# Block-sparse attention and a GELU MLP on one core: weights loaded between batch 0 and batch 1, masks of batch 1 turned by TensorE, casts on GpSimd, key sums from the key transposes

## The chip, the core and the metric

The kernel runs on one core of one Trainium2 chip. The metric is the time of the whole program on the device in microseconds, as the median of several runs. Beside it stands one profiled execution, which gives start, length and waits of every instruction. A compute core has five engines that run side by side, each working through its own instructions in order: TensorE (PE in the profile; its weight loads are PEld), VectorE (DVE), ScalarE (ACT), GpSimd (POOL) and SyncE (SP), which here only issues transfers. An engine that waits for one instruction holds up everything behind it.

## What is computed

Block-sparse causal attention over 4 batches, 8 heads, 768 positions and head width 64, followed by a two-layer MLP without biases:

```python
k_rep = k.reshape(B, H, 12, 64, D).mean(axis=3)          # one key mean per block of 64
gate_scores = einsum('bhsd,bhnd->bhsn', q, k_rep)        # per query and block
gate_scores = where(causal, gate_scores, -1e9)
top_idx = argsort(gate_scores)[..., -3:]                 # the 3 best blocks
mask = (chosen blocks, and the own block) & (i >= j)
scores = where(mask, q @ k.T / sqrt(D), -1e9)
attn = softmax(scores)
x = (attn @ v), heads side by side                       # 3072 x 512
h = x @ w_in                                             # 3072 x 2048
out = gelu_tanh(h) @ w_out                               # 3072 x 512
```

q, k, v, w_in, w_out and the output are fp32. The kernel multiplies in fp16 but takes the gate scores in fp32, since they decide which blocks are chosen.

## The kernel before, in words

Two heads make a pair; there are 16 pairs, four to a batch, so pair 4 is the first of batch 1. For each pair `pre` (line 342) prepares, `heads2` (batch 0) or `heads` (batches 1 to 3) computes the attention, and `turn_out` (673) turns the normalised result into xT, the MLP's input. For each batch `s1` (791) is the first MLP layer with GELU (128 matmuls, of 512 and of 256 columns in turn, L798) and `s2` (822) the second (96 matmuls, L829). s1 of a batch starts when the last exponential of its attention is done; the attention of the next batch starts when nearly all of s1 has been multiplied. s2 of one batch is filler for TensorE during the attention of the next.

*No order is written out by hand.* Every piece of work is an `Op` with a cost for each engine that may do it, its dependencies, a priority, and the PSUM bank it takes. `Plan.solve` (52) simulates all engines by these costs, takes the ready operation of the best priority at each step, picks the engine that ends first, and emits all operations in the order of their planned starts. So a changed cost changes the order of many instructions and the engine of some. The costs are plans only; on the chip an instruction waits for its real operands, in the fixed order of its engine.

*Loading.* `load` (215) issues k, q and v of a pair from SyncE. Pairs of batch 0 come in rows of 64 values and are turned by TensorE (`turn`, 351, into PSUM, with copies out of it in `turned`). Later pairs come as blocks of 32 x 32 in four transfers each for k and q (`emit_t`), and DVE's 32 x 32 transpose (`tr`, 374, shown as L378) finishes the turn. k and q have four buffers each, v three.

*Key sums and gates.* In batch 0 the sums of each block of 64 keys are six more fp32 matmuls a pair with an indicator matrix `ind` (L361), behind the second half of the key transposes. In later batches DVE adds them up (`ks_all`, L400). `ksb_m` (L418) spreads them over the two heads, `gate` (L455) multiplies them with the queries, DVE turns the scores (L468) and picks the three best blocks (`sel_e`, L474 to 487), which leaves an additive mask, `madd`.

*Masks.* The mask must be turned so that it can stand beside the queries as extra rows. In batch 0 TensorE does it (`mask`, L508), in the later batches a transposing DMA from SyncE (`mask_dma`, L516), and `mc` copies twelve rows for each head into qT.

*Casts.* `cast_v` makes v fp16 on DVE. The fp16 casts of keys (`kc_all`) and queries (`q16`) go to DVE or ScalarE.

*Attention.* Scores (L589, L729), exponential on ScalarE (L603, L742), the causal triangle cut by GpSimd (L629, L756), multiplication with v (L642, L768), and normalisation on DVE (L667, L668).

*Weights.* `load_w` (258) issues them from GpSimd, with a cast to fp16 during the transfer: w_in in two parts during batch 0, w_out in one piece when v of pair 5 has arrived. A small copy of v, `after` (L264), makes GpSimd wait for that arrival. `hold` (271) is a tiny transfer from SyncE that reads the first part of w_in; it holds SyncE's queue, and so all loads of batch 1, until that part is there.

*Warm-up.* `warm` (859) offers 110 matmuls without use of the worst priority, with which TensorE passes the time while it has nothing else.

Of the kernel before, what the change touches and what calls it, by code (L numbers as in the profile page):

```python
# [8 lines left out]
FP32 = mybir.dt.float32  # L9
# [113 lines left out]
def kernel(  # L123
# [22 lines left out]
    HALF = S // 2  # L146

# [15 lines left out]
    ident32 = const.tile([128, 128], FP32)  # L163
# [3 lines left out]
    bmask = const.tile([128, 2, 16], FP32)  # L167
    nc.vector.memset(bmask, 0.0)
# [6 lines left out]
    ks16 = [const.tile([128, 16], FP32, name=f"ks16_{i}") for i in range(NK)]  # L175
    for i in range(NK):
        nc.vector.memset(ks16[i], 0.0)
    start = gtp.tile([128, NF, S], FP16, tag="gT", name="start")
# [36 lines left out]
    def load(p, key, held=None, prio=None):  # L215
        b, hp = divmod(p, HP)

        def emit(_):
            sd = (iov if key == "v" else io).tile(
                [128, NC, 2, 64], FP32, tag=key, name=f"{key}_sd_{p}")  # L220
            for hh in range(2):
                nc.sync.dma_start(
                    out=sd[:, :, hh, :],
                    in_=SRC[key][b, 2 * hp + hh].rearrange(
                        "(c p) d -> p c d", p=128))
            T[key, p] = sd
        def emit_t(_):

            sd = io.tile([128, NC * 4, 32], FP32, tag=key, name=f"{key}_sd_{p}")
            for hh in range(2):  # L230
                for a in range(2):
                    nc.sync.dma_start(  # L232
                        out=sd[64 * hh + 32 * a:64 * hh + 32 * a + 32],
                        in_=SRC[key][b, 2 * hp + hh].rearrange(
                            "(t i) (a j) -> a i t j", i=32, j=32)[a])
            T[key, p] = sd
        dve = key != "v" and p >= HP
        go = add({SP: 2.0 if dve else 1.0}, emit_t if dve else emit,
                 [free_sd.get((key, p - (PV if key == "v" else PF))), held]
                 + moved[-3:-2],  # L240
                 prio=10 * p if prio is None else prio)
        issued[key, p] = go
        ld[key, p] = add({"DMA": 2.5 if dve else 1.8},
                         lambda _: None, [go],
                         prio=1000 * b + hp, lag=1.6)
        moved.append(ld[key, p])

    def cast_v(p, old):
        b, hp = divmod(p, HP)

        def emit(eng):
            copy(eng, v16[p % NB][:, :, :, 0:64], T["v", p])
        free_sd["v", p] = ld["v16", p] = add(
            {DVE: 0.47}, emit,
            [ld["v", p], old],
            prio=1000 * (b - 1) + 599 + hp if b else 100 * hp - 55)

    def load_w(name, dst, src, cols, deps, prio, after=None):
        view = src.rearrange("(i p) f -> p i f", p=128)

        def emit(_):
            if after is not None:
                x = const.tile([1, 16], FP32, name="after")
                nc.gpsimd.tensor_copy(out=x, in_=T[after][0:1, 0, 0, 0:16])  # L264
            nc.gpsimd.dma_start(out=dst[:, :, cols], in_=view[:, :, cols])
        go = add({POOL: 1.3}, emit, deps, prio=prio)
        n = dst.shape[1] * (cols.stop - cols.start)
        return add({"DMA": 12.0 * n / 8192}, lambda _: None, [go], prio=prio,
                   lag=1.6)

    def hold(dep):
        def emit(_):
            x = const.tile([1, 16], FP16, name="held")
            nc.sync.dma_start(out=x, in_=w_in16[0:1, 0, 0:16])
        return add({SP: 0.5}, emit, [dep], prio=-1)
# [3 lines left out]
    def consts():  # L279
        def ind(_):  # L280
            T["ind"] = x = const.tile([128, NC, 16], FP32, name="ind")
            nc.gpsimd.memset(x, 1.0)
            nc.gpsimd.affine_select(
                out=x, in_=x, compare_op=ALU.is_ge, fill=0.0,
                base=0, pattern=[[128, NC], [-64, 16]], channel_multiplier=1)
            nc.gpsimd.affine_select(
                out=x, in_=x, compare_op=ALU.is_ge, fill=0.0,
                base=63, pattern=[[-128, NC], [64, 16]], channel_multiplier=-1)
        c_E["ind"] = add({POOL: 1.2}, ind, [], prio=-60)

# [51 lines left out]
    def pre(p):  # L342
# [8 lines left out]
        def turn(key, a):  # L351
            def emit(_):
                w = plan.buf["w" + key, p, a]
                for c in range(3):
                    nc.tensor.transpose(  # L355
                        w[:, c * 128:(c + 1) * 128],
                        T[key, p][:, 3 * a + c].rearrange("p h d -> p (h d)"),
                        ident32)
                if key == "k" and a == 1:
                    for c in range(NC):  # L360
                        nc.tensor.matmul(  # L361
                            w[:, 384:400],
                            T["k", p][:, c].rearrange("p h d -> p (h d)"),
                            T["ind"][:, c, :], start=(c == 0),
                            stop=(c == NC - 1))
            return emit

        def turned(key, a, dst):
            def emit(eng):
                copy(eng, dst()[:, a * HALF:(a + 1) * HALF],  # L370
                     plan.buf["w" + key, p, a][:, 0:HALF])
            return emit
# [10 lines left out]
        if first:  # L383
            for a in range(2):
                t = add({PE: 0.33 + 0.7 * a}, turn("k", a),
                        [ld["k", p], c_E["ind"]], pr,
                        takes=("pre", ("wk", p, a)))
                kcs.append(add({DVE: 0.52, ACT: 0.5},
                               turned("k", a, lambda: kT2[i]), [t], pr,
                               gives=[] if a else [("wk", p, a)]))  # L390
                if a == 1:
                    free_sd["k", p] = t
                    ksr.append(t)
        else:
# [16 lines left out]
            kcs = [add({DVE: 0.56, ACT: 0.84}, kc_all(h),  # L411
                       [t, old.get("k", None)], pr + 0.1) for h in range(2)]

        def ksb_m(_):
            T["ksb", p] = hd.tile([128, 2, 16], FP32, tag="ksb",
                                  name=f"ksb_{p}")
            src = plan.buf["wk", p, 1][:, 384:400] if first else ks
            nc.vector.tensor_tensor(  # L418
                out=T["ksb", p], in0=bmask,
                in1=src.unsqueeze(1).to_broadcast([128, 2, 16]),  # L420
                op=ALU.mult)
        ksb = add({DVE: 0.15}, ksb_m, ksr, pr)
        if first:
            add({"NONE": 0.0}, lambda _: None, [ksb] + kcs, pr,
                gives=[("wk", p, 1)])
# [4 lines left out]
        if first:  # L430
# [5 lines left out]
            for a in range(2):  # L436
                t = add({PE: 0.33}, turn("q", a), [ld["q", p]], pr,
# [3 lines left out]
                qcs.append(add({DVE: 0.52, ACT: 0.5}, turned("q", a, q32),  # L441
# [19 lines left out]
        g = add({PE: 0.45}, gate, [ksb] + qcs, pr, takes=("pre", ("gt", p)))  # L461
# [30 lines left out]
        if first:  # L492
            def q16(eng):
                copy(eng, qT2[i], T["qT32", p])
            q16s = [add({DVE: 0.5, ACT: 0.8}, q16, qcs, pr + 0.1)]
# [24 lines left out]
        if first:  # L520
            m = add({PE: 0.28}, mask, [sel], pr, takes=("pre", ("mk", p)))
# [4 lines left out]
            mcs = [add({DVE: 0.55, ACT: 0.7}, mc2, [m], pr,  # L526
                       gives=[("mk", p)])]
            rdy[p] = kcs + q16s + mcs + [c_E["E"]]
        else:
            go = add({SP: 1.2}, mask_dma, [sel], -50)  # L530
            m = add({"XBAR": 0.8}, lambda _: None, [go], pr, lag=2.5)

            def mc(h):
                def emit(eng):
                    copy(eng, qT16[i][h][64:76, 128:S],
                         T["mT", p][64 * h:64 * h + 12, :])
                return emit
            mcs = [add({DVE: 0.33}, mc(h), [m, old.get("s")], pr)
                   for h in range(2)]
# [32 lines left out]
    def heads2(p):  # L572
# [4 lines left out]
        for ui, unit in enumerate(UNITS):  # L577
# [30 lines left out]
            ex = add({ACT: 0.1 + 2 * n * 0.000833}, ex_e,  # L608
# [25 lines left out]
            for h in range(2):  # L634
# [15 lines left out]
                pvs[h].append(add({PE: 0.03 * n / 128 + 0.05}, pv_e,  # L650
# [22 lines left out]
    def turn_out(p, norms, base):  # L673
# [23 lines left out]
        if p >= HP + 2:  # L697
            go = add({SP: 1.2}, ot_dma, norms, -50)
            x = add({"XBAR": 0.8}, lambda _: None, [go], base - 20, lag=2.5)
        else:  # L700
            ot = add({PE: 0.33}, ot_e, norms, base + 50,
# [120 lines left out]
    def s2(b):  # L822
        kind = "ops" if b < B - 1 else "tail"
        prev = None
        for ti in range(NC):
            mm = prev
            for f in range(NF):
                def mm_e(_, ti=ti, f=f):
# [6 lines left out]
                         [mm, gelus[b][f], w_ready["out"]],  # L835
# [23 lines left out]
    def warm():  # L859
        z = ident16.unsqueeze(1).to_broadcast([128, 2, 128])  # L860
        for n in range(110):
# [3 lines left out]
            add({PE: 0.107}, emit, [], 1e6, takes=("warm", ("warm", n)),  # L865
# [11 lines left out]
    for p in range(HP):  # L877
        pre(p)
    for x in range(2):
        w_ready["in", x] = load_w(  # L880
            "in", w_in16, moe_w_in, slice(DFF // 2 * x, DFF // 2 * (x + 1)),
            [ld["v", 2]], 30 + x)
    held = hold(w_ready["in", 0])
    for p in range(HP):
        heads2(p)
    s1(0)
    for p in range(HP, NPAIR):
# [6 lines left out]
        if p == HP + 1:  # L894
            w_ready["out"] = load_w("out", w_out16, moe_w_out, slice(0, DM),
                                    [ld["v", HP + 1]], 30, ("v", HP + 1))
            s2(0)
# [39 lines left out]
```

The softmax here doesn't subtract the row's maximum and nothing guards it: scores larger than these inputs give would overflow.

## Time and profile before

| What | Value |
|---|---|
| time, median of 3 runs (lowest to highest) | 289.04 us (287.75 to 289.88) |
| span of the profiled execution | 288.1 us |
| TensorE busy | 268.4 us, 93% of the span |
| of it the warm-up matmuls (L863) | 18.3 us |
| ScalarE, VectorE, GpSimd busy | 180.9, 134.4, 51.4 us |
| mean granted TensorE clock | 0.974 |
| transfers | 33.68 MB, nearly all packets under 512 bytes |

The busy share is a mean over stages with different limits. The stages can be read off the chain of work that ended last:

| Stage | Stretch, us | TensorE busy, us |
|---|---|---|
| first loads and warm-up | 0 to 8.8 | 6.9, all of it warm-up |
| batch 0: preparation and attention | 8.8 to 46.65 | nearly all, with 7.7 of warm-up |
| s1 of batch 0 | 46.65 to 84.5 | 28, with 3.5 of warm-up |
| attention of batch 1, s2 of batch 0, then s1 of batch 1 | 84.5 to 149.67 | 61.3 |
| attention of batch 2, s2 of batch 1 | 149.67 to 186.89 | nearly all |
| s1 of batch 2 | 186.89 to 207.80 | all |
| attention of batch 3, s2 of batch 2 | 207.80 to 243.84 | all |
| s1 and s2 of batch 3, last store | 243.84 to 288.1 | 40.6 |

The stretches of s1 in batches 0 and 2 hold the same multiplications. The page's granted clock (PEclk) is in tenths of full speed; some matmul records can be missing, so counts may be a little low.

### The profile page before, as it was taken

How to read it: one execution, taken by the hardware profiler on the slowest of the kernel's cores; microseconds unless marked ns; L12 is line 12 of the kernel's file. 1: busy time of each engine (PE TensorE's matmuls, PEld its weight loads, DVE VectorE, ACT ScalarE, POOL GpSimd, SP SyncE). 2: the span in 40 equal slices, each digit the busy share in tenths (PEclk: the TensorE clock that was granted, in tenths of full speed). 3: DMA queues.
4: the chain of work that ended last, by engine and by line, in shares of the span. 5: the costliest groups of instructions: out<-in, count | busy, mean ns of one | idle time of the engine just before them, and what ended most of it. 6: DMA issues, size and time to landing. Idle time of an engine off the chain costs nothing.

```text
span 288.1 us, 5862 instructions
## 1 busy us (share of the span) xinstructions
PE 268.4 (93%) x2278; PEld 157.3 (55%) x2278; DVE 134.4 (47%) x449; ACT 180.9 (63%) x232; POOL 51.4 (18%) x121
## 2 busy tenths in 40 slices
PE   7999999990799999949999999999999999999994
PEld 5886657650355665425555664455556654665441
DVE  0368887832661987977614998840023320000000
ACT  2267789842479989674578995356699942664111
POOL 8305332200003334000004451000034410000000
PEclk9999999997599999997999999999999999999998
DMA  8991999999873999999994332460011321000111
GB/s 187 267 204 11 208 171 170 161 185 193 145 134 68 153 208 188 178 166 205 176 186 109 84 91 71 116 84 0 0 39 30 89 68 74 36 2 0 73 75 73
DMA packets 135596, 33.68 MB, mean 117 GB/s; under 512 B 129424, under 2 KB 131472, under 8 KB 135568
## 3 DMA queue, kind: packets, MB, share of 16 engines
q1 hardware_dynamic: 132448, 29.11, 50.6%
q0 software_dynamic: 3120, 4.19, 8.8%
q8 instruction: 18, 0.29, 0.4%
q14 instruction: 10, 0.08, 0.1%
HBM read 27.26 MB, written 6.29 MB: 116 GB/s over the span
## 4 chain that ended last, share of the span: by engine, by line
PE 79%; SPq 5%; DVE 5%; DMA 5%; ACT 3%; issue 2%; POOL 1%; DVEq 0%; ACTq 0%; POOLq 0%
PE wide L798 26%; PE bank L829 24%; PE wide L729 8%; PE bank L768 5%; PE bank L863 5%; SPq L232 4%; PE wide L589 4%; DMA mT<-madd 2%; PE bank L355 2%; PE bank L642 2%; PE bank L455 2%; PE bank L361 2%; DMA q_sd<-in_q_dram 2%; ACT at L742 1%; SPq L516 1%
## 5 line engine op out<-in xcount | busy, mean ns | idle before, releaser
L829 PE MATMUL bank<-w_out,gT 128*128 128x512 f16 x384 | 99.5, 379 | 0.0
L798 PE MATMUL wide<-xT,w_in 128*128 128x512 f16 (+1 forms) x512 | 89.0, 334 | 0.0
L811 ACT ACTIVATE gT<-wide 128x768 f16<-128x768 f32 x64 | 51.4, 809 | 35.2 <-PE wide L798 35.2
L798 PEld LDWEIGHTS <-w_in 128*128 128x128 f16 x512 | 50.7, 100 | 36.6 <-issue 5.0
L742 ACT ACTIVATE at<-wide 128x896 f16<-128x896 f32 x72 | 61.8, 914 | 5.0 <-PE wide L729 2.0
L756 POOL TENSOR_SCALAR_AFFINE_SELECT at<-at 128x256 f16<-128x256 f16 x72 | 31.0, 431 | 147.0 <-ACT at L742 146.9
L829 PEld LDWEIGHTS <-gT 128*128 128x128 f16 x384 | 36.2, 98 | 31.4 <-issue 0.5
L729 PE MATMUL wide<-qT,kT 76*128 76x512 f16 (+1 forms) x192 | 39.0, 305 | 0.0
L202 ACT COPY osb<-bank 128x512 f32<-128x512 f32 x19 | 11.1, 582 | 32.4 <-PE bank L829 31.9
L768 PEld LDWEIGHTS <-at 128*128 128x128 f16 x504 | 23.5, 97 | 9.8 <-POOL at L756 2.4
L768 PE MATMUL bank<-v,at 128*128 128x65 f16 x504 | 27.1, 194 | 0.2 <-POOL at L756 0.2
L729 PEld LDWEIGHTS <-kT 76*128 76x128 f16 x192 | 18.2, 97 | 15.1 <-issue 0.2
L603 ACT ACTIVATE at<-wide 128x1024 f16<-128x1024 f32 (+1 forms) x24 | 20.8, 919 | 4.3 <-PE wide L589 4.2
L455 PE MATMUL bank<-qT,ksb 128*32 128x160 f32 x128 | 7.9, 321 | 13.6 <-DVE ksb L418 13.6
L863 PE MATMUL bank<-ident 128*128 128x256 f16 x110 | 18.3, 303 | 1.8 <-DVE ident L166 1.8
L668 DVE TENSOR_TENSOR xn<-bank,zr 128x384 f16<-128x384 f32 x32 | 17.8, 557 | 1.1
L206 DVE COPY qT<-mT 12x640 f16<-12x640 f16 x24 | 7.8, 324 | 21.0 <-DMA mT<-madd 20.8
L202 ACT CAST kT<-kT 64x768 f16<-64x768 f32 x13 | 10.8, 829 | 9.0 <-DVE kT L378 8.9
L206 DVE COPY osb<-bank 128x512 f32<-128x512 f32 x5 | 3.4, 689 | 27.0 <-ACT at L742 18.7
L667 DVE RECIPROCAL zr<-bank 128x6 f32<-128x6 f32 x32 | 6.1, 190 | 19.3 <-PE bank L768 17.8
L378 DVE STREAM_TRANSPOSE qT<-q_sd 128x768 f32<-128x768 f32 x12 | 11.6, 969 | 5.8 <-DMA q_sd<-in_q_dram 5.7
L863 PEld LDWEIGHTS <-ident 128*128 128x128 f16 x110 | 11.4, 110 | 4.8 <-DVE ident L166 1.8
(71 smaller groups left out, 212.7 us busy)
## 6 DMA issues: line engine op xcount, KB each, us to landing
v_sd<-in_v_dram SPq DMA_DIRECT2D x32, 192.0 KB, 3.2
out_dram<-osb SPq DMA_DIRECT2D x24, 256.0 KB, 2.2
k_sd<-in_k_dram SPq DMA_DIRECT2D x48, 96.0 KB, 3.0
q_sd<-in_q_dram SPq DMA_DIRECT2D x48, 96.0 KB, 2.8
w_in<-in_moe_w_in_dram POOLq DMA_DIRECT2D x2, 1024.0 KB, 10.8
w_out<-in_moe_w_out_dram POOLq DMA_DIRECT2D x1, 2048.0 KB, 17.0
k_sd<-in_k_dram SPq DMA_DIRECT2D x8, 192.0 KB, 3.4
q_sd<-in_q_dram SPq DMA_DIRECT2D x8, 192.0 KB, 3.5
```

What stands on the lines that cost most here:

```text
L202: nc.scalar.copy(out=out, in_=in_)
L455: nc.tensor.matmul(g[32 * j:32 * j + 32, 0:160].rearrange("g (c t) -> g c t", t=32), T["ksb", p].rearrange("p h n -> p (h n)"), q5[:, j], ...
L603: nc.scalar.activation(out=T["at", u][:, :, 0:n], in_=plan.buf[("st",) + u].rearrange("p (h w) -> p h w", h=2)[:, :, 0:n], func=AF.Exp, bi ...
L668: nc.vector.tensor_tensor(out=T["xn", p][:, :, h, :], in0=pvv[:, :, 0:64], in1=zr.to_broadcast([128, NC, 64]), op=ALU.mult)
L729: nc.tensor.matmul(st[:, x:e], kT16[i][h][0:76, s0:s0 + 128], qT16[i][h][0:76, s0 + (x - cb):s0 + (e - cb)], start=True, stop=True)
L742: nc.scalar.activation(out=T["at", u][:, 0:n], in_=plan.buf[("st",) + u][:, 0:n], func=AF.Exp, bias=0.0, scale=SCALE)
L756: nc.gpsimd.affine_select(out=dg, in_=dg, compare_op=ALU.is_ge, fill=0.0, base=0, pattern=[[0, 2], [1, 128]], channel_multiplier=-1)
L768: nc.tensor.matmul(pvv[:, qc, 0:65], at[:, cb + (qc - jc) * 128: cb + (qc - jc + 1) * 128], v16[i][:, jc, h, :], start=(gi == 0 and jc == ...
L798: nc.tensor.matmul(hps[:, u:e], w_in16[:, ci, f * 128:(f + 1) * 128], T["xT", b][:, ci, u:e], start=(ci == 0), stop=(ci == HP - 1))
L811: nc.scalar.activation(out=T["gT", b][:, f, :], in_=plan.buf["hps", b, f][:, 0:S], func=AF.Gelu_apprx_tanh, bias=0.0, scale=1.0)
L829: nc.tensor.matmul(plan.buf["ops", b, ti], T["gT", b][:, f, ti * 128:(ti + 1) * 128], w_out16[:, f, :], start=(f == 0), stop=(f == NF - 1))
L863: nc.tensor.matmul(plan.buf["warm", n][:, 0:256], ident16, z, start=True, stop=True)
```

## The change

It has four parts that the title names, and changed costs in the planner.

1. *Weights.* w_in (two parts by columns) and w_out (now two parts by rows) are issued together, when v of pair 3 has arrived. SyncE's queue is held until the first part of w_out is there. All weights are thus to travel between the loads of batch 0 and those of batch 1, and s2 of batch 0 is planned without waiting for a late w_out.
2. *Masks.* The pairs of batch 1 have their masks turned by TensorE as batch 0 does, which takes four transposing DMAs off SyncE. The last xT of every batch is also turned by TensorE.
3. *Casts.* v is cast on GpSimd, keys on DVE or GpSimd, and the queries of pairs 1 to 3 on GpSimd. This frees DVE and ScalarE.
4. *Key sums of batch 0.* The key transposes become fp32 matmuls with an identity that is widened by two columns of ones for the two blocks of 64 (`identk`, 130 columns). The sums then come out beside each transposed block, and the matmuls with `ind` and GpSimd's making of it fall away. DVE spreads the sums in two halves.

The rest is in the costs: loads of later batches are planned with 3.0 us to landing, the first 18 warm-up matmuls with the slow clock's price, and 96 of them are offered instead of 110.

```diff
+    NCOLD = 18
+    LAND = 3.0
+    NWARM = 96
+    identk = const.tile([128, 130], FP32, name="identk")
+    ident32 = identk[:, 0:128]
+    nc.vector.memset(identk[:, 128:130], 0.0)
+    nc.vector.memset(identk[0:64, 128:129], 1.0)
+    nc.vector.memset(identk[64:128, 129:130], 1.0)
...
-                 + moved[-3:-2],
+                 + moved[-2:-1],
-        ld[key, p] = add({"DMA": 2.5 if dve else 1.8},
-                         lambda _: None, [go],
-                         prio=1000 * b + hp, lag=1.6)
-        moved.append(ld[key, p])
+        move = add({"DMA": 2.5 if dve else 1.75}, lambda _: None, [go],
+                   prio=1000 * b + hp)
+        moved.append(move)
+        ld[key, p] = add({"NONE": 0.0}, lambda _: None, [move],
+                         prio=1000 * b + hp, lag=LAND if b else 1.6)
...
         free_sd["v", p] = ld["v16", p] = add(
-            {DVE: 0.47}, emit,
+            {POOL: 0.85}, emit,
...
-            nc.sync.dma_start(out=x, in_=w_in16[0:1, 0, 0:16])
+            nc.sync.dma_start(out=x, in_=w_out16[0:1, 0, 0:16])
...
                 for c in range(3):
-                    nc.tensor.transpose(
-                        w[:, c * 128:(c + 1) * 128],
-                        T[key, p][:, 3 * a + c].rearrange("p h d -> p (h d)"),
-                        ident32)
-                if key == "k" and a == 1:
-                    for c in range(NC):
-                        nc.tensor.matmul(
-                            w[:, 384:400],
-                            T["k", p][:, c].rearrange("p h d -> p (h d)"),
-                            T["ind"][:, c, :], start=(c == 0),
-                            stop=(c == NC - 1))
+                    src = T[key, p][:, 3 * a + c].rearrange(
+                        "p h d -> p (h d)")
+                    if key == "k":
+                        nc.tensor.matmul(w[:, c * 130:(c + 1) * 130], src,
+                                         identk, start=True, stop=True)
+                    else:
+                        nc.tensor.transpose(w[:, c * 128:(c + 1) * 128], src,
+                                            ident32)
...
-            kcs = [add({DVE: 0.56, ACT: 0.84}, kc_all(h),
+            kcs = [add({DVE: 0.56, POOL: 0.85}, kc_all(h),
                        [t, old.get("k", None)], pr + 0.1) for h in range(2)]
...
-            q16s = [add({DVE: 0.5, ACT: 0.8}, q16, qcs, pr + 0.1)]
+            q16s = [add({POOL: 0.85} if p else {DVE: 0.56}, q16, qcs, pr + 0.1)]
...
-            go = add({SP: 1.2}, mask_dma, [sel], -50)
-            m = add({"XBAR": 0.8}, lambda _: None, [go], pr, lag=2.5)
+            byPE = p < 2 * HP
+            if byPE:
+                m = add({PE: 0.44}, mask, [sel], pr, takes=("pre", ("mk", p)))
+            else:
+                go = add({SP: 1.2}, mask_dma, [sel], -50)
+                m = add({"DMA": 0.8}, lambda _: None, [go], pr, lag=4.0)
...
-        if p >= HP + 2:
+        if p >= HP + 2 and hp != HP - 1:
...
-        for n in range(110):
+        for n in range(NWARM):
...
     for x in range(2):
         w_ready["in", x] = load_w(
-            "in", w_in16, moe_w_in, slice(DFF // 2 * x, DFF // 2 * (x + 1)),
-            [ld["v", 2]], 30 + x)
-    held = hold(w_ready["in", 0])
+            "in", w_in16, moe_w_in,
+            (every, every, slice(DFF // 2 * x, DFF // 2 * (x + 1))),
+            [ld["v", 3]], -200 + x, None if x else ("v", 3))
+    for x in range(2):
+        w_ready["out", x] = load_w(
+            "out", w_out16, moe_w_out,
+            (every, slice(NF // 2 * x, NF // 2 * (x + 1)), every),
+            [issued["in"]], 40)
+    held = hold(w_ready["out", 0])
     for p in range(HP):
         heads2(p)
     s1(0)
+    s2(0)
...
-        if p == HP + 1:
-            w_ready["out"] = load_w("out", w_out16, moe_w_out, slice(0, DM),
-                                    [ld["v", HP + 1]], 30, ("v", HP + 1))
-            s2(0)
```

## The prediction, made before the changed kernel ran

> **What bounds the kernel now.** I read the page first, by slices (its second part), then the chain of waits, then tables by stage, then the DMA queue's own timeline.
>
> ```profile
> PE   7999999990799999949999999999999999999994
> ...
> PEclk9999999997599999997999999999999999999998
> DMA  8991999999873999999994332460011321000111
> ```
>
> Forty slices of 7.2 us. TensorE is busy nearly always, so the kernel is bound by TensorE's work plus the holes in it: the front, slices 9 and 10 (64.8 to 79.2 us), slice 18, the tail. The clock row sinks behind both inner holes. The DMA row is full from 29 us to 158 us.
>
> ```profile
> 46.50:64.20 17.70, 17.68 (x141) 1.00 1.07 168
> 64.20:74.10 9.90, 0.04 (x4) 0.70 1.17 194
> 74.10:79.50 5.40, 5.40 (x27) 0.60 0.69 116
> ...
> 125.00:129.20 4.20, 0.47 (x10) 1.00 0.94 186
> 129.20:137.00 7.80, 7.80 (x42) 0.78 1.04 204
> ```
>
> TensorE alone by stretches: length, busy time, granted clock, DMA share, GB/s. 9.9 us stand still, then 5.4 us run at 0.60 (2.2 us lost). A second hole loses 3.7 us, and 7.8 us behind it run at 0.78 (1.7 us lost). Together 17.5 us.
>
> ```profile
> 58.30 0.51 SPq L232
> 58.87 4.44 SPq L232
> 63.36 2.77 SPq L232
> 66.17 4.98 DMA q_sd<-in_q_dram
> 71.23 0.40 issue
> 71.63 0.98 DVE qT L378
> 72.61 0.83 DVE ks L400
> 73.45 0.46 DVE qT L206
> 74.06 0.76 PE bank L455 x8
> ```
>
> The chain of waits (start, length). The hole ends with the gate matmuls of pair 6 (L455). They waited for DVE's key sums, and those stand behind the transpose of pair 6's queries, whose load crawled.
>
> ```profile
> 34.97 5.12 SPq L232 DMA_DIRECT2D k_sd<-in_k_dram  x4
> 40.18 2.36 SPq L232 DMA_DIRECT2D q_sd<-in_q_dram  x4
> ...
> 58.30 10.98 SPq L232 DMA_DIRECT2D q_sd<-in_q_dram  x4
> ```
>
> The sync engine's timeline. Four such DMAs take 2.4 us to issue when the engines keep up; they took 10.98 us while w_out was in flight (issued at 53.1, landed 17.0 us later). The first load of batch 1 met the second half of w_in in the same way: 5.12 us.
>
> **What the Trainium skill says.** "DMA: Bandwidth & Descriptors", SWDGE vs HWDGE vs iDMA: transfers issued from GpSimd and from sync sit in different queues of the same engines, which take turns. The 10.98 us agree: a weight transfer slows every load beside it. "TensorE: Matmul & The Clock Gate", Part 1: an idle window of about 3.4 us halves the clock, and about as long a busy one restores it. Both dips above follow idle stretches of that length or more. "GPSIMD Engine Reference", 3.1: a Q7 loop takes 1.03 to 1.8 cycles an element with one input, 2.6 with two, at 1.2 GHz. No cast of this size runs on GpSimd before; its 64x768 select took 0.90 us, between the two one-input figures. "SBUF — State Buffer", Who interferes with whom: a VectorE copy or cast in a two-port mode and a GpSimd instruction lock each other out for a whole instruction. No wait before shows it; from now on it can.
>
> **The change, part by part.**
>
> *Warm-up and key sums (batch 0).* 42 warm matmuls stand ahead of the first key transpose, from 1.84 to 8.79 us. The first key load is issued by 1.85 us, and the slowest key load landed 4.7 us after its issue, so it was there by 6.6 us: the warm-up held it back. In the new order 25 stand there. 42 in 7.0 us, at the planner's 0.107 us warm and twice that cold, means 23 cold; 25 then end near 7.1 us: 1.7 us earlier. Key sums: 6 matmuls with `ind` took 1.25 us, and six transposes 0.66 us, a pair. The new form is six fp32 matmuls of 130 columns. L455 (160 fp32 columns, two passes, 321 ns a record, against about 178 ns of fixed latency read from the 256- and 512-column rows) gives 0.9 ns a column and pass, so 0.23 us each, 1.40 us a pair. That saves 0.5 us a pair, 2.0 us in all. Pair 0's saving is on the path; of the rest I count 0.9 us, since ScalarE (busy about 5 us in 6 there) shares the limit. First MLP matmul of batch 0: 46.65 - 1.7 - 0.5 - 0.9 = 43.5 us.
>
> *Weights.* Both matrices now go as four parts of 1 MB, issued from GpSimd behind a copy that waits for v of pair 3, and the sync queue is held for the third. That wait has the masking of pair 1 behind it; v of pair 3 lands near 22 us and masking of pair 1 came at 31.1, so it costs nothing. GpSimd reaches the issue behind pair 0's last masking (26.1 us before, some 2 us earlier now, less three new casts): 24.5 to 26. w_in's first part took 8.2 us alone, and in 28.8 to 36 us the queues moved 208 GB/s, so 1.05 MB a further 5.0 us: the hold opens at about 25 + 8.2 + 10 = 43 us, 8 us later than before. Contention with the last part is 6 us, as before (seven loads in 19.8 us against 13.6 at 0.57 us a DMA). From then on a pair needs ten DMAs, 5.7 us.
>
> Pair by pair, with 3.2 us to landing: queries of pair 4 are there at 54, the gate stands in the new order behind 70 MLP matmuls, at 43.5 + 2.8 (wait for the last xT, as before) + 70 x 0.16 = 57.5. Pair 5: there at 60, transposed and summed by 63, due at 64. Pair 6: 66, ready at 70, due at 71. So the loads are just in time, and 20 us of MLP fill the gap that stood empty. The stage from the first MLP matmul to batch 1's heads: 128 x 0.16 = 20.5, plus 2.8 wait, plus two gates (0.82) and two masks (0.88) = 25.0 us. It was 37.85 (46.65 to 84.5): 12.9 us less, the heart of the change.
>
> *Masks of batch 1 by TensorE.* Four DMA transposes leave the sync queue (1.2 to 3.3 us each), and DVE no longer waits for them with other work behind (15.1 us of waits from 46 to 130). Cost: 4 x 0.44 us of TensorE, and two copies a pair, half of them on ScalarE, beside matmuls. The last xT of batches 1 to 3 also goes to TensorE, 0.45 us each.
>
> *Batch 1's heads, s2(0) and s1(1).* Now 84.5 to 149.67, 65.2 us. The undisturbed like stage, 207.80 to 243.84, takes 36.0 us without gates, 0.96 us of it MLP matmuls of the next stage: 35.1. Add two masks 0.9, four gates 1.6, three turned outputs 1.35: 39.0, and s1(1) with two late gates 21.3. For GpSimd I add 2 us, below: 62.3, a gain of 2.9. It is what the second hole and its cold stretch cost, less the added matmuls.
>
> *Casts on GpSimd.* DVE loses 16 v casts (8.7 us) and the key casts it did (6.3 us), ScalarE up to 10.8 us; none of this was the end of the chain but for the key casts ahead of gates. Behind each cast on GpSimd stands the masking of probabilities (L756, 0.43 us), and a PV matmul waits for that with TensorE's whole queue behind it. Price: floor 0.66 us, ceiling 1.9 us (two-input loop[...]); I take 1.1, the 0.90 of the select with a wider input. The planner reckons with 0.85, so each slips 0.25, plus waits for the port, and 15 casts stand among the maskings of batches 1 and 2. About half delay one: 2 us in batch 1, 1 us in batch 2.
>
> *Rest.* Batch 2's heads, 37.2 us, + 0.45 + 1 = 38.7; batch 3's + 0.45; MLP stages and tail unchanged.
>
> Sum: -3.1 - 12.9 - 2.9 + 1.5 + 0.45 = -17 us: 289 - 17 = **272 us**.
>
> **The rivals.**
>
> *The weights delay batch 1 instead.* If a part takes half of w_out's 17.0 us, the hold opens at 25 + 8.2 + 17 = 50, 7 us later, and pair 4's gate is due 3.5 us after its data at best. So 4 us of stall, as much again at the pairs behind, and 2 us of cold clock: 282 us. For it: 8.2 us is one sample. Against it: w_out's 17 us shared the engines with loads, and nothing else runs in 25 to 43 now.
>
> *GpSimd becomes the bound (slower).* At 1.9 us, seven casts in batch 0 and fifteen later each run 1.05 us over plan, 23 us if all are exposed: 272 - 3 + 23 = 292 us. For it: TensorE's order is fixed, and DVE's own casts lock the port. Against it: in a heads stage GpSimd is busy 10 of 36 us, and the 0.90 us row.
>
> *Cleaner than forecast.* Casts hide (-3), and batch 0, freed of casts on ScalarE and DVE, ends 3 us earlier: 266 us.
>
> **How the numbers follow.** Forecast 0.56, late batch 1 0.20, slow GpSimd 0.08, cleaner 0.16. Range 265 to 284: it takes in the cleaner case and most of the late one. Faster by over 1% (below 286.1): all but the slow case and the worst of the late one, 0.89; within 1%, 0.03; slower, 0.08.
>
> **What would show it.** Right: no TensorE hole over 3 us between 45 and 130, clock 1.0 there; no load of batch 1 near 10 us to issue; first key transpose near 7 us; the MLP of batch 0 starting near 43.5; heads of batch 1 near 68.5. Wrong: gates waiting for key sums around 57 to 71 us (late weights), PV weight loads waiting for GpSimd by more than a few us in total, casts over 1.3 us, or a first hole between the warm-up and the first key.

## The result, and the profile after

| | before | changed |
|---|---|---|
| time, median (lowest to highest), us | 288.8 (287.75 to 289.88) | 276.29 (275.88 to 276.4) |
| ratio, with its 95% interval | | 0.9564 (0.9527 to 0.9601) |
| span of the profiled execution, us | 288.1 | 274.6 |
| TensorE busy, us | 268.4 | 264.7 |
| mean granted clock | 0.974 | 1.0 |

The change saves 12.5 us, 4.4%. The forecast was 272 us; the direction and the main cause held, the size was 4.3 us too good. One execution of the kernel with the old weights (288.65 us) and one of the second group without casts on GpSimd (277.27 us) ran over 1.5% longer than the fastest of their kernel, and the medians and ratios below leave these two out.

The page's slices of the changed kernel, now 6.9 us each:

```profile
PE   6999899999999999799999999999999999999994
...
PEclk9999999999999999999999999999999999999999
DMA  8996999999999999999999233300022122000222
```

The two inner holes and both dips of the clock are gone; slice 17 is a small new hole. The DMA row stays nearly full up to 151 us, and the loads of batch 1 now run beside TensorE's work instead of ahead of it. TensorE alone, by stretches of the changed kernel (length, busy time, clock, DMA share, GB/s):

```profile
60.00:80.00 20.00, 19.97 (x167) 1.00 1.18 157
...
113.30:115.01 1.71, 0.00 (x0) 1.00 1.23 278
```

SyncE's timeline shows when the hold opened and how the loads of batch 1 then ran:

```profile
43.58 0.62 SPq L283 DMA_DIRECT2D held<-w_out  x1
44.30 4.45 SPq L241 DMA_DIRECT2D k_sd<-in_k_dram  x4
48.85 2.36 SPq L241 DMA_DIRECT2D q_sd<-in_q_dram  x4
...
71.56 4.07 SPq L241 DMA_DIRECT2D q_sd<-in_q_dram  x4
```

The longest issue of a load of batch 1 is 4.45 us; it was 10.98. The gates of pairs 4 and 5 on TensorE's timeline:

```profile
58.59 0.48 PE L465 MATMUL bank<-qT,ksb 128*32 128x160 f32 x8
...
65.67 0.48 PE L465 MATMUL bank<-qT,ksb 128*32 128x160 f32 x8
```

Neither row carries an idle time in brackets: these gates, forecast for 57.5 and 64, do not wait. Stage by stage, each stage counted from its first row on TensorE's timeline (the table ahead of the prediction took its bounds from the chain of waits, which puts some of them up to 0.6 us later):

| Stage | before, us | changed, us | forecast, us |
|---|---|---|---|
| start to first key transpose | 8.8 | 6.1 | 7.0 |
| batch 0, to the first matmul of s1 | 37.7 | 37.8 | 36.5 |
| s1 of batch 0, to the heads of batch 1 | 37.8 | 26.0 | 25.0 |
| heads of batch 1, s2(0), s1(1) | 64.7 | 63.8 | 62.3 |
| heads of batch 2, s2(1), s1(2) | 58.6 | 60.2 | 59.6 |
| heads of batch 3 and the end | 80.5 | 80.7 | 80.7 |

11.9 of 13.5 us come from the third row. The fifth has become slower.

### The profile page after: what moved, and what is told of

It is laid out like the page before. It is cut to its first block, busy times and chain, and to the rows that moved or that the text cites. A ratio compares the mean times of both kernels' runs of the same rounds, so it can differ in the third digit from the quotient of the medians.

```text
span 274.6 us, 5892 instructions
## 1 busy us (share of the span) xinstructions
PE 264.7 (96%) x2278; PEld 153.7 (56%) x2278; DVE 130.3 (47%) x437; ACT 172.5 (63%) x221; POOL 81.0 (29%) x155
## 5 line engine op out<-in xcount | busy, mean ns | idle before, releaser
L819 PE MATMUL wide<-xT,w_in 128*128 128x512 f16 (+1 forms) x512 | 86.2, 326 | 1.7 <-ACT gT L832 1.7
L819 PEld LDWEIGHTS <-w_in 128*128 128x128 f16 x512 | 49.4, 98 | 35.6 <-issue 3.1
L763 ACT ACTIVATE at<-wide 128x896 f16<-128x896 f32 x72 | 62.4, 917 | 6.3 <-PE wide L750 2.5
L777 POOL TENSOR_SCALAR_AFFINE_SELECT at<-at 128x256 f16<-128x256 f16 x72 | 31.7, 446 | 80.6 <-ACT at L763 78.8
L750 PEld LDWEIGHTS <-kT 76*128 76x128 f16 x192 | 17.5, 97 | 14.3 <-issue 0.4
L213 POOL CAST kT<-kT 64x768 f16<-64x768 f32 x17 | 14.0, 823 | 26.5 <-DVE kT L376 23.5
L213 POOL CAST v<-v_sd 128x768 f16<-128x768 f32 x16 | 14.1, 883 | 19.2 <-DMA v_sd<-in_v_dram 17.9
L884 PE MATMUL bank<-ident 128*128 128x256 f16 x96 | 15.8, 293 | 2.1 <-DVE ident L170 2.1
L376 DVE STREAM_TRANSPOSE kT<-k_sd 128x768 f32<-128x768 f32 x12 | 11.7, 974 | 10.8 <-DMA k_sd<-in_k_dram 10.7
L494 DVE MAX8 mx<-gm 128x8 f32<-128x12 f32 x160 | 13.1, 157 | 0.6
## 6 DMA issues: line engine op xcount, KB each, us to landing
w_out<-in_moe_w_out_dram POOLq DMA_DIRECT2D x2, 1024.0 KB, 19.6
```

Of the source, the lines that this page charges most:

```text
L213: nc.gpsimd.tensor_copy(out=out, in_=in_)
L376: nc.vector.transpose(out=T[key + "T32", p], in_=T[key, p].rearrange("p t j -> p (t j)"))
L750: nc.tensor.matmul(st[:, x:e], kT16[i][h][0:76, s0:s0 + 128], qT16[i][h][0:76, s0 + (x - cb):s0 + (e - cb)], start=True, stop=True)
L763: nc.scalar.activation(out=T["at", u][:, 0:n], in_=plan.buf[("st",) + u][:, 0:n], func=AF.Exp, bias=0.0, scale=SCALE)
L777: nc.gpsimd.affine_select(out=dg, in_=dg, compare_op=ALU.is_ge, fill=0.0, base=0, pattern=[[0, 2], [1, 128]], channel_multiplier=-1)
L819: nc.tensor.matmul(hps[:, u:e], w_in16[:, ci, f * 128:(f + 1) * 128], T["xT", b][:, ci, u:e], start=(ci == 0), stop=(ci == HP - 1))
```

## The experiments

All times are medians; ratios are against the kernel before, measured on the same chip beside it. It took 289.75, 289.24 and 289.63 us in the three groups of experiments, so kernels of different groups are compared by their ratios, of which 1% is 2.9 us. The last column names the group.

| Kernel | us | ratio (95%) | group |
|---|---|---|---|
| weights alone | 280.63 | 0.9692 (0.9637 to 0.9748) | 1 |
| weights and last xT | 279.75 | 0.9678 (0.9629 to 0.9726) | 2 |
| changed, old weights | 283.12 | 0.9795 (0.9726 to 0.9863) | 1 |
| changed, masks by DMA | 281.29 | 0.9694 (0.9641 to 0.9747) | 1 |
| changed, last xT by DMA | 276.3 | 0.9542 (0.9497 to 0.9587) | 2 |
| changed, key sums by `ind` | 276.43 | 0.9546 (0.951 to 0.9582) | 2 |
| changed, old warm-up | 278.13 | 0.9614 (0.9578 to 0.9649) | 2 |
| changed, once more | 276.78 | 0.9563 (0.9527 to 0.9598) | 3 |
| weights, masks, last xT, planner's costs | 275.78 | 0.9507 (0.9474 to 0.954) | 3 |
| changed, no casts on GpSimd | 274.04 | 0.9471 (0.9407 to 0.9536) | 1 |
| the same, once more | 273.53 | 0.9446 (0.9413 to 0.9479) | 3 |
| the same, loads planned at 3.2 us | 271.92 | 0.9392 (0.9361 to 0.9423) | 3 |

**The weights alone.** The kernel before with w_in moved behind v of pair 3, and with:

```diff
+    for x in range(2):
+        w_ready["out", x] = load_w("out", ..., [issued["in"]], 40)
+    held = hold(w_ready["out", 0])
...
+    s2(0)
```

Expected: 

> The kernel before with the weights part alone: four parts of 1 MB issued behind v of pair 3, SyncE held for the first part of w_out, s2 of batch 0 planned without a late w_out. Theory (the collision of w_out with batch 1's loads was nearly the whole loss): the 9.9 us hole and its slow clock go, about 277 us. Rival 1 (the hole was DVE standing behind mask transposes and casts, which this leaves in place): 284 to 289 us, with a hole still at the gates of batch 1.

Measured: 280.63 us, 9 us below the kernel before. The first hole is gone: from the first s1 matmul to the heads of batch 1 it takes 28.3 us instead of 37.8. But TensorE's waits show a new one later, and SyncE's timeline shows its cause:

```profile
PE wide L797 <- DMA xT<-xn: 5.7, 2, 5.3
```
```profile
113.18 0.47 SPq L847 DMA_DIRECT2D out_dram<-osb  x1
113.75 1.43 SPq L689 DMA_TRANSPOSE xT<-xn  x1
```

The first row says that the MLP of batch 1 waited twice, up to 5.3 us, for the transposing DMA of its last xT, until 117.47 us. The data of that DMA were ready at 106.4 us; it was issued at 113.75, behind loads and stores in SyncE's one queue. So the theory held for the first hole, and its 277 us failed because the kernel then ran into the next wait.

**The weights and the last xT.** Added to the former:

```diff
-        if p >= HP + 2:
+        if p >= HP + 2 and hp != HP - 1:
```

Expected: 

> The kernel before with the weights part and the last xT of each batch turned by TensorE, nothing else. Theory (those two take away the two big waits): the 5.3 us wait goes, 275 to 277 us, as fast as the whole change. Rival (the masks by DMA hold VectorE and make another hole in its place): 279 to 281 us.

Measured: 279.75 us, a ratio like that of the weights alone; the rival was right. The waits from 100 to 130 us, and SyncE's timeline:

```profile
DVE qT L206 <- DMA mT<-madd: 5.1, 1, 5.1
...
PE bank L454 <- DVE qT L377: 4.6, 1, 4.6
```
```profile
119.52 2.53 SPq L515 DMA_TRANSPOSE mT<-madd  x2
```

VectorE stood 5.1 us at the copy of a mask that was ready by 113.8 us and whose transposing DMA was issued late, at 119.5 us. The transpose of the last pair's queries (L377) waited behind it, and the last gate behind that. Removing one wait on SyncE's queue exposed another of about the same size.

**The old weights in the changed kernel.** The first experiment's inverse: w_in in two parts, w_out in one piece behind v of pair 5, `hold` on w_in.

Expected: 

> The changed kernel with the weights loaded as before (w_in in two parts, w_out in one piece behind v of pair 5, SyncE held for w_in's first part); masks, casts, key sums and warm-up as changed. Theory: the hole comes back, 286 to 290 us. Rival 1: most of the gain stays, about 279 us, since DVE and SyncE are relieved.

Measured: 283.12 us, between the theory's 286 and the rival's 279 us. By the ratios the weights are worth 6.7 us in this company and the other parts together 5.9 us without them, both with about 2 us of play. Its waits and SyncE's timeline (from the longest execution, of 287.0 us span; the others spanned 281.3 to 283.8, so the waits there are likely shorter):

```profile
PE bank L466 <- DVE ksb L430: 9.3, 2, 8.3
```
```profile
56.72 8.34 SPq L231 DMA_DIRECT2D v_sd<-in_v_dram  x2
65.16 6.52 SPq L241 DMA_DIRECT2D k_sd<-in_k_dram  x4
```

The crawl beside w_out and the hole at a gate are back, on other loads. The mean granted clock was 0.988 in each of the other three executions, against 0.999 to 1.0 in the changed kernel.

**Masks of batch 1 by DMA.**

```diff
-            byPE = p < 2 * HP
+            byPE = False
```

Expected: 

> The changed kernel with the masks of batch 1 turned by DMA transposes from SyncE, as before. Theory: 4 x 0.44 us of TensorE are saved, SyncE and the loads of batch 1 become about 5 us later, DVE waits for the transposes: 277 to 281 us. Rival 1 (masks by TensorE are a main part of the gain): 284 us or more, with a hole at a gate of batch 1.

Measured: 281.29 us, just above the theory's range. By the ratios the masks are worth 3.8 us here, with 2 us of play. No single long hole takes their place: TensorE's longest waits are 2.05, 1.62 and 1.64 us at a gate, a PV and an s2 matmul. The stages put the loss before and after batch 1: 28.2 us instead of 26.0 from s1 of batch 0 to the heads of batch 1, and 62.7 instead of 60.2 in batch 2. What lies behind each wait was not isolated.

**The last xT by DMA.** The one-line edit above, undone in the changed kernel.

Expected: 

> The changed kernel with the last xT of batches 1 to 3 turned by DMA again. Theory (the transpose stands in SyncE's full queue, and the first MLP matmuls of batch 1 wait for it, as the 5.3 us wait in the kernel with the weights alone shows): a hole of 2 to 5 us before s1 of batch 1, 278 to 281 us. Rival (only the combination with late masks made that hole): 275 to 276.5 us, since 1.35 us of TensorE are saved.

Measured: 276.3 us. The rival was right: a wait of 1.68 us for the transpose exists, but it stands where the changed kernel waits 1.72 us for something else.

**Key sums by `ind`.** Six transposes and six narrow matmuls a pair again.

Expected: 

> The changed kernel with the key sums of batch 0 by the indicator matmuls again (six transposes and six narrow fp32 matmuls a pair instead of six of 130 columns). The prediction's step: 2.0 us of TensorE saved in batch 0, 1.4 of them on the path, so 277.7 us here. Theory after the trace (batch 0 took 37.8 us with and without the saving, since TensorE, ScalarE and VectorE wait for each other there): within 0.5 us of the changed kernel, about 276.3.

Measured: 276.43 us. Batch 0 in three kernels (length, then busy time of PE, PEld, DVE, ACT, POOL), first before, then changed, then this one:

```profile
8.79:46.65 37.86, 37.53 (x497) 26.82 (x496) 27.61 (x109) 27.13 (x37) 10.68 (x19) 1.00 0.87 169
```
```profile
6.14:43.97 37.83, 36.73 (x478) 24.73 (x476) 23.47 (x104) 26.28 (x37) 18.96 (x37) 1.00 1.12 191
```
```profile
6.10:44.09 37.99, 37.75 (x494) 26.28 (x493) 23.37 (x100) 26.21 (x37) 20.20 (x37) 1.00 1.12 193
```

The lengths agree to 0.2 us. Over all profiled executions batch 0 took 37.3 to 38.6 us, with either form of the sums. The key sums save work and no time that shows. One reason: 7.9 us of TensorE's busy time in batch 0 of the kernel before, and 8.3 us in the changed one, are warm-up matmuls, so TensorE had time to spare there.

**The old warm-up.**

```diff
-    NCOLD = 18
-    NWARM = 96
+    NCOLD = 0
+    NWARM = 110
```

Expected: 

> The changed kernel with the warm-up matmuls offered as before (110, all at the fast clock's price in the planner), so that more of them stand ahead of the first key transpose. Theory: the first key transpose moves from 6.1 to about 8.5 us and the end by as much, 278.5 us. Rival: the loads of the later pairs set batch 0's pace, and the front is given back there, 276.5 us.

Measured: 278.13 us, near the theory. The first key transpose moves to 8.99 us. The earlier front is worth 1.4 to 1.8 us; the intervals of the two ratios overlap, so this is likely, not certain. The changed kernel run once more had its first key transpose at 7.33 instead of 6.14 us. That was not the load: the first key loads, issued by 1.85 us, landed at most 3.3 us after their issue in both. The same 25 warm-up matmuls took 5.43 us instead of 4.25, and the transposes follow them without a pause.

**No casts on GpSimd.**

```diff
-            {POOL: 0.85}, emit,
+            {DVE: 0.56}, emit,
...
-            kcs = [add({DVE: 0.56, POOL: 0.85}, kc_all(h),
+            kcs = [add({DVE: 0.56, ACT: 0.84}, kc_all(h),
...
-            q16s = [add({POOL: 0.85} if p else {DVE: 0.56}, q16, qcs, pr + 0.1)]
+            q16s = [add({DVE: 0.56, ACT: 0.84}, q16, qcs, pr + 0.1)]
```

Expected: 

> The changed kernel with the casts of v on VectorE and those of keys and queries on VectorE or ScalarE, none on GpSimd. Theory (GpSimd casts are worth little, since the waits of TensorE on GpSimd are about what DVE and ScalarE gain): 275 to 279 us. Rival 2 (casts on GpSimd carry a part of the gain by freeing DVE): 281 us or more. Rival 3 (they cost, because they delay the maskings and lock VectorE's port): 273 us or less.

Measured: 274.04 us, below the changed kernel and between theory and rival 3. So both ran side by side:

Expected of the changed kernel: 

> The changed kernel once more, so that it stands beside the next three on the same chip: 276.3 us.

Expected of this one: 

> The changed kernel without casts on GpSimd once more. Theory (the casts delay the maskings, lock VectorE's port and cost about 2 us in the attention of batches 1 and 2): 274 us, 2 us below the changed kernel. Rival (the 274.0 us seen before was the chip or the run): equal to the changed kernel within 0.5 us.

Measured: 276.78 and 273.53 us, and the two intervals are apart. So the casts on GpSimd, with the order that the planner makes of them, cost 3 us. By the stages of the table above, from these two profiles: batch 1 takes 62.4 us with them and 61.0 without, batch 2 60.7 and 58.6; s1 of batch 0 is shorter with them, 26.0 against 26.8. TensorE's weight loads for PV, from 60 to 175 us, waited longer in total for GpSimd's masking, first in the changed kernel, then without the casts:

```profile
PEld L789 <- POOL at L777: 4.9, 14, 0.8
```
```profile
PEld L789 <- POOL at L777: 2.3, 7, 0.5
```

One place of the changed kernel shows how such a wait comes about (all engines, start and length, one row of each):

```profile
96.10 0.83 POOL L213 CAST v<-v_sd 128x768 f16<-128x768 f32 x1 [0.51 <-DMA v_sd<-in_v_dram]
...
96.30 0.67 DVE L429 TENSOR_TENSOR ksb<-bmask,ks 128x32 f32<-128x32 f32 x1
...
96.87 1.08 POOL L777 TENSOR_SCALAR_AFFINE_SELECT at<-at 128x256 f16<-128x256 f16 x2
...
97.33 0.39 PE L789 MATMUL bank<-v,at 128*128 128x65 f16 x7 [0.19 <-POOL at L777]
```

The cast of v waited 0.51 us for its load with the whole GpSimd queue behind it, then ran 0.83 us. The masking came only then, and the PV matmul waited for it, 0.19 us here. Beside it VectorE's small product, which reads two operands from SBUF, took 0.67 us. Its mean in the changed kernel, then without casts on GpSimd:

```profile
L429 DVE TENSOR_TENSOR ksb<-bmask,ks 128x32 f32<-128x32 f32 x12 | 3.3, 277 | 0.1
```
```profile
L429 DVE TENSOR_TENSOR ksb<-bmask,ks 128x32 f32<-128x32 f32 x12 | 2.1, 174 | 0.1
```

277 against 174 ns for the same twelve instructions (235 in the changed kernel's repeat, 202 in the kernel before). That agrees with the Trainium skill, "SBUF — State Buffer", Who interferes with whom: a VectorE instruction with two SBUF inputs contends with a GpSimd instruction that reads SBUF, and one waits for the end of the other. VectorE's own casts of keys, of which the prediction had said that they and GpSimd may lock each other out, grow too:

```profile
L215 DVE CAST kT<-kT 64x768 f16<-64x768 f32 x7 | 5.0, 719 | 0.1
```
```profile
L215 DVE CAST kT<-kT 64x768 f16<-64x768 f32 x8 | 4.4, 547 | 0.1
```

The first row is the changed kernel (745 ns in its repeat), the second the one without casts on GpSimd. How the 3 us split between the later maskings and the longer VectorE instructions was not isolated.

**Weights, masks and last xT only.** The changed kernel with casts, key sums and warm-up as before; the planner's new costs stay. A version built up from the kernel before with its old costs was not run.

Expected: 

> Only the weights, the masks of batch 1, the last xT by TensorE and the planner's costs as changed; casts, key sums and warm-up as before. Theory (these carry the whole gain but the earlier front): 276 us, the front's 2 us and the casts' loss of 2 us cancelling. Rival (freeing VectorE and ScalarE by casts and key sums is needed to use the time): 279 us or more.

Measured: 275.78 us. These three parts, with the planner's new costs, carry the whole gain. Early front and key sums add about 2 us (273.53), though the intervals overlap by a hair, and the casts on GpSimd take 3 us away (276.78). What the new costs do alone stays open.

**Loads planned at what they take.** On top of no GpSimd casts:

```diff
-        move = add({"DMA": 2.5 if dve else 1.75}, lambda _: None, [go],
+        move = add({"DMA": 3.2 if dve else 1.75}, lambda _: None, [go],
```

Expected: 

> The changed kernel without casts on GpSimd, and with 3.2 us for a k or q load in the planner instead of 2.5 (the trace showed 8.2 us from pair to pair in batch 1, the planner reckons with 6.75), so that gates and late casts are placed where the data arrive. Theory: the rest of the waits for late loads goes, 272 to 273.5 us. Rival (the order without GpSimd casts has no wait left that this could take): 274 us, or more if the new order is worse.

Measured: 271.92 us, the fastest here, 17.7 us below the kernel before. After the start TensorE's longest wait in its profile is 0.2 us. Against 273.53 us the intervals of the ratios overlap a little (0.9423 and 0.9413), so the last 1.6 us are likely, not certain; 0.8 us of the difference between the two profiles lies in the warm-up, which ended at 6.31 and at 7.07 us.

## Why the prediction was right, and where its sizes were off

*Weights: right, but for the pace of the loads.* The hold was worked out to open at 43 us and opened at 43.58. Contention over the first seven loads was put at 6 us, and it was 5.9 (19.6 us against 13.7). The stage was put at 25.0 us and took 26.0: the multiplications of s1 took 21.0 us instead of 20.5, what stands among them until the last xT is turned 3.15 instead of 2.8, and two matmuls of s2 0.43, less 0.3 at the masks. Weights alone brought 9 us and their removal cost 6.7, so the cause is shown from both sides. What failed is "From then on a pair needs ten DMAs, 5.7 us": the keys of pairs 6 to 9 were issued at 60.93, 68.12, 77.23 and 84.39 us, so 7.2 to 9.1 us apart, although the last weights had landed by about 50 us. The gates of pairs 4 and 5 did not wait all the same. The step also left out that the 12.9 us cannot be had with the weights alone: in the two kernels without the masks by TensorE a wait of about 5 us appears later, each time behind a transposing DMA in SyncE's queue.

*Key sums: the cost was right, its worth wrong.* The step gave 1.40 us for a pair's six matmuls; in the changed kernel pair 0's stand from 6.14 to 7.49 us, 1.35. But "pair 0's saving is on the path; of the rest I count 0.9 us" failed: 1.4 us were counted and none came. Batch 0 took 37.8 us against 37.7. Neither the experiment with `ind` nor the stage table gives it anything. The step took saved TensorE time as saved time where about 8 us of TensorE's time were warm-up; and ScalarE, put at 5 us in 6, was busy 27.1 of 37.9 us. One wait there can be named; the chain that holds the whole stage at 37.8 us was not isolated:

```profile
30.24 0.84 POOL L213 CAST start<-qT 128x768 f16<-128x768 f32 x1
30.60 0.97 DVE L486 TENSOR_TENSOR gm<-gx,cgate 128x120 f32<-128x120 f32 x1
```
```profile
33.19 0.45 PE L520 MATMUL bank<-ident,madd 128*128 128x128 f16 x5 [0.75 <-DVE madd L499]
```

The sum of the gate scores of pair 3 took 0.97 us beside a GpSimd cast, against 0.30 us in the mean before, and TensorE waited 0.75 us for the mask that follows.

*Warm-up: right, the size in part luck.* 1.7 us were forecast, 2.65 came in the profiled run and 1.5 in the repeat. The prediction took the pace of the warm-up matmuls as fixed, but 25 of them took 4.2 to 5.5 us over nine executions, and the 42 ahead of the kernel before's transposes took 7.11 us in its profile, 6.54 and 6.04 in the two kernels with the weights moved. The gain in the profiled run covered the missing 1.4 us of the key sums, so the start of s1 (43.97 against 43.5) looked right by two errors that cancel.

*Heads of batch 1 and s1(1): 62.3 forecast, 63.8 measured (62.4 in the repeat).* 1.7 us of it (0.7 in the repeat) is a wait behind the late load of pair 11, which the prediction did not price. ScalarE's and TensorE's timelines:

```profile
113.43 0.83 ACT L211 CAST qT<-qT 64x768 f16<-64x768 f32 x1 [2.26 <-DVE qT L376]
114.16 1.49 ACT L832 ACTIVATE gT<-wide 128x768 f16<-128x768 f32 x2
```
```profile
115.01 2.11 PE L819 MATMUL wide<-xT,w_in 128*128 128x512 f16 x12 [1.72 <-ACT gT L832]
```

A cast of queries stood on ScalarE ahead of the first GELUs of batch 1. VectorE had waited 1.69 us for the keys of pair 11, until 108.67 us, and turned the queries behind them without a pause, at 112.42; so the cast's data came late, the GELUs could not free PSUM, and s1 stopped. In the kernel without casts on GpSimd this wait is gone, with the loads still planned at 2.5 us.

*Casts on GpSimd: the loss right in size, by luck.* 3 us were charged (2 in batch 1, 1 in batch 2), and the casts cost 3 us (about 1.4 and 2.1, less 0.9 gained in the stage of s1(0)). But the way to it failed. 1.1 us was taken for a cast; they measured 0.82 us (64 rows) and 0.88 (128 rows), about what the planner reckons with, so the slip over plan from which the charge was worked out was nearly nil. What the runs show instead are maskings behind casts that wait for a load, and VectorE instructions that take longer beside GpSimd. The sign that was named for trouble, PV weight loads waiting for GpSimd by more than a few us, came in part: 4.9 us, against 2.4 in the kernel before. The relief of VectorE and ScalarE, which the prediction gave no gain of its own, was indeed not needed: the kernels without those casts are faster.

*The rest.* Batch 2 came 0.6 us over its forecast; the casts took about 2 us there where 1 was charged. Another 0.8 us is a slip in the base: the forecast took 17 us off the median of 289.04 us, but the stages from which the 17 us come were read in an execution of 289.87 us. Summed: 0.5 at the start, 1.0 in s1(0), 1.5 in batch 1, 0.6 in batch 2 and 0.8 in the base give the 4.3 us but for rounding.

## What to carry to other kernels

When one queue carries loads, stores and transposes, removing its longest wait can expose the next, as it did twice here, so try the parts together as well as alone before judging any of them. A cast moved to an engine with time to spare is not free if that engine's queue also holds work on which the bound engine waits: see what each cast waits for, and what stands behind it. Work saved on the busiest engine counts only where that engine sets the length of the stage; look first how much of its busy time is filler.

## What the runs showed of the hardware that had not been expected

VectorE instructions stretch beside GpSimd casts: products of 128x32 with two operands in SBUF from 174 ns in the mean to 235 and 277, casts of keys from 547 to 719 and 745, and one sum of gate scores took 0.97 us, against 0.30 in the mean before. The same 25 warm-up matmuls took from 4.2 to 5.5 us in different executions, and the first key transpose moved with them (6.14 and 7.33 us in two executions of one kernel). Four loads of k or q took 2.2 to 4.7 us to issue from 60 to 100 us, with no weights in flight, so that 2.4 us is not a price for a stretch in which the DMA row is full.
